# 64-row transposes, strided fills for the gate, zero products and a new instruction order in a block-sparse attention and Fourier-mixing kernel

## The chip, the cores and the metric

The kernel runs on one core of a Trainium2 chip. The metric is the device time of one execution in microseconds. Before the change it is 297.08 us, the median of three runs (296.85 to 297.6).

A core has five engines that work side by side: TensorE (PE in the profile, with its weight loads as a row of its own, PEld), VectorE (DVE), ScalarE (ACT), GpSimd (POOL) and SyncE (SP), which here only issues transfers. Each works off its own queue in order and waits on semaphores for the others. TensorE multiplies into PSUM; the other engines copy from PSUM to SBUF.

## The reference

The program is an attention over selected key blocks, followed by a Fourier-mixing layer with an MLP. Cut to what matters (4 batches, 8 heads, 768 positions, head size 64, model size 512):

```python
# attention, per batch and head; 12 blocks of 64 keys
k_rep = k.reshape(B, H, 12, 64, D).mean(axis=3)
gate = q @ k_rep.T                       # 768 x 12
gate = where(block_of_query >= key_block, gate, -1e9)
selected = top 3 blocks of gate, and the query's own block
scores = 0.125 * q @ k.T, where selected and causal, else -1e9
attn_out = softmax(scores) @ v
# mixing, per batch, on x = heads side by side (768 x 512)
mixed = real(fft over model axis of fft over sequence axis of x)
u = x + mixed
un = (u - mean) / sqrt(var + 1e-6)
out = u + relu(un @ w_ch1) @ w_ch2       # 512 -> 2048 -> 512
```

## The kernel before, in words

Two heads make a pair; there are 16 pairs, four to a batch. Pairs 0 to 6 (P below `NX` = 7) and pairs 7 to 15 take two forms of the same stages, told below.

**Loads and transposes.** `load` brings q and k of a pair in fp32 as six blocks of 128 positions by 128 columns (two heads of 64). `a_tp` (line 286) turns each with a TensorE transpose into a PSUM tile `tp` of 128 by 768: six products of 128 rows per tile (line 292), two tiles per pair. `a_sums` (line 297) sums the keys by block of 64 on VectorE, `a_half` puts the sums into the weights of the gate, `a_k` copies the keys to fp16 on ScalarE (lines 308, 311), `a_q32` copies the queries to fp32 on VectorE (line 316), and `a_q` casts them to fp16 on GpSimd.

**Gate.** `g_mm` multiplies queries with block sums, in four groups of 32 columns of the array. `g_turn` transposes the result on VectorE to the tile `gt`, and bounds the blocks that lie ahead of the query: for pairs 0 to 6 by a minimum with a table `lim` (line 351), for the later pairs by three strided fills. `g_max` finds the eight largest values of each row in nine or ten instructions. `g_less` has two steps: j = 0 writes 1 where a block is below the third largest (`is_lt`), and j = 1 multiplies by a table `oth` or `oth2` that holds -60000 everywhere but at the query's own block. So the mask `lt` is 0 for a block that counts and -60000 for one that does not. `g_back` transposes it back to `mt`.

**Scores.** `s_mm` computes six PSUM tiles of scores per pair, up to two banks each, that hold scores transposed (keys on the partitions). For pairs 0 to 6 each head's product takes 64 rows of the array, the two heads on the two halves (line 409), and the mask is added by more 64-row products with an indicator of blocks, `indz` (line 421). For the later pairs `stage_K` copies the mask beside the queries on GpSimd, and one product of 96 rows does both (line 414). `s_exp` is the exponential on ScalarE (line 431), `s_sel` cuts the causal triangle on GpSimd, `v_mm` multiplies with v and a column of ones in 42 products (line 449), and `v_x` divides, on VectorE, into the tile `x_b` of the batch.

**Mixing.** For each batch `fold_s`, `fold_d` and `fg` fold the sequence and model axes by symmetry on VectorE; `y_mm` and `m_mm` are the two transforms; `m_u` adds x, `m_x` centres and scales it on ScalarE. For batch 0 `t_mm` transposes it on TensorE (24 products, line 585) and `t_copy` copies it to `unT` on VectorE; for the other batches a DMA does this. `w1_mm` then makes 16 tiles `h` of the hidden layer (eight products each, lines 629 and 631), `w1_relu` brings them to SBUF, `w2_mm` multiplies with w_ch2 (lines 648 and 656), `w2_o` adds u on VectorE and `w2_out` stores.

**Order.** All of this is issued in an order that is written out by hand as the string `ORDER`: each word is a step and its arguments (`tk:4` the transposes of pair 4's keys, `s:3,2` its score tile 2, `w:1,5` a tile of W1 in batch 1). `WORK` maps words to functions. Each engine's queue holds its instructions in this order. All PSUM tiles come from one pool of four buffers of two banks each (`pst`), so that a step which takes a new tile waits until the tile four before it is read out.

Of the kernel before, what the change touches and what calls it, by code (L numbers as in the profile page):

```python
# [11 lines left out]
FP = mybir.dt.float32  # L12
F16 = mybir.dt.float16
# [15 lines left out]
def _consts_np():  # L29
# [22 lines left out]
    oth = np.where(np.arange(9)[:, None] + 3 != nn, NEG, 0.0)[None].repeat(128, 0)  # L52

    lim = np.where(nn[None, 4:8] > np.arange(3, 7)[:, None], -3e38, 3e38)
    lim = lim.reshape(1, 16).repeat(128, 0).astype(np.float32)

    indc = np.zeros((4, 32, 2, NB), np.float32)
    for g in range(4):
        for n in range(NB):
            indc[g, n, g % 2, n] = 1.0  # L60

    own = 2 * np.arange(5)[None, :] + 2 + (p // 64)[:, None]
    oth2 = np.zeros((128, 5, 2, 16), np.float32)
# [47 lines left out]

ORDER = """
Lk:1 Lq:1 Lk:2 Lq:2 tk:0 ks:0 tq:0 Lq:3 Lk:3 kh:0 qc:0 iz:1 tk:1 qs:0 kc:0 g:0 ks:1 iz:0 gt:0 tq:1
kc:1 gx:0 Lq:4 Lv:0 Lk:4 Lv:1 kh:1 gl:0,0 tk:2 gl:0,1 gm:0 kc:2 qc:1 s:0,3 s:0,2 ks:2 e:0,3 qs:1
tq:2 Lq:5 Lk:5 s:0,5 qc:2 g:1 e:0,5 e:0,2 kh:2 s:0,4 gt:1 qs:2 s:0,0 e:0,4 gx:1 s:0,1 d:0,2 tq:3
gl:1,0 e:0,0 gl:1,1 tk:3 gm:1 e:0,1 d:0,0 qc:3 g:2 d:0,3 kc:3 d:0,5 s:1,5 gt:2 d:0,4 s:1,0 e:1,5
qs:3 ks:3 s:1,4 e:1,0 tq:4 d:0,1 gx:2 vc:0 e:1,4 s:1,3 qc:4 s:1,1 Lv:2 e:1,3 s:1,2 gl:2,0 kh:3
tk:4 gl:2,1 e:1,2 d:1,3 gm:2 g:3 d:1,4 ks:4 d:1,0 v:0 d:1,5 gt:3 vc:1 kc:4 gx:3 e:1,1 s:2,5 Lv:3
Lq:6 LF:0 Lq:7 Lk:6 Lk:7 LT:0 s:2,3 kh:4 gl:3,0 e:2,5 gl:3,1 s:2,4 e:2,3 d:1,1 x:0 tq:5 qs:4 e:2,4
g:4 d:2,3 gm:3 qc:5 s:2,0 d:2,4 s:2,2 d:1,2 e:2,0 gt:4 d:2,5 tk:5 vc:2 gx:4 e:2,2 s:2,1 ks:5 d:2,0  # L120
Lv:4 Lq:8 Lk:8 s:3,1 e:2,1 v:1 gl:4,0 kh:5 gl:4,1 kc:5 d:2,1 gm:4 d:2,2 s:3,2 x:1 e:3,1 vc:3 g:5
e:3,2 Lv:5 Lc:0 d:3,1 s:3,5 gt:5 s:3,0 fs:0,1 e:3,5 s:3,3 d:3,2 gx:5 e:3,0 s:3,4 fs:1,1 tq:6
gl:5,0 e:3,3 fs:0,0 v:2 gl:5,1 fs:1,0 e:3,4 d:3,3 qc:6 d:3,0 s:4,5 x:2 d:3,4 s:4,4 e:4,5 d:3,5
s:4,0 qs:5 v:3 e:4,0 gm:5 fs:2,0 fs:2,1 e:4,4 s:5,5 x:3 s:4,1 e:5,5 s:5,1 e:4,1 fd:2,0 s:4,2 s:5,0
fs:3,1 e:5,1 fs:3,0 s:5,2 fd:2,1 e:5,0 fd:3,1 s:4,3 fd:3,0 e:5,2 tk:6 f:0,1 f:0,2 e:4,3 Lk:9 Lq:9
tk:7 f:0,3 e:4,2 f:0,0 y:0,1 ks:7 pg:0 W:0 kc:6 y:0,0 tr:0,1 d:4,0 kc:7 d:4,4 d:4,5 ks:6 d:5,5
d:4,1 ty:0,1 tr:0,0 s:5,3 d:5,2 s:5,4 d:4,3 kh:6 W:1 ty:0,0 m:0,2 qs:6 e:5,3 u:0,2 m:0,1 vc:4
e:5,4 m:0,0 u:0,1 xu:0,2 d:5,4 tk:8 d:5,1 d:4,2 u:0,0 xu:0,1 d:5,0 xt:0,2 W:2 g:6 un:0,2 xu:0,0
xt:0,1 gt:6 tq:8 un:0,1 kc:8 xt:0,0 qc:8 tq:7 un:0,0 qs:8 v:4 Lq:10 Lk:10 Lv:6 Lq:11 qc:7 bn:0,3
w:0,4 d:5,3 qs:7 bn:0,1 w:0,5 r:0,4 gx:6 ks:8 w:0,6 r:0,5 gl:6,0 kh:7 gl:6,1 x:4 w:0,7 r:0,6 gm:6  # L130
w:0,3 r:0,7 s:6,5 r:0,3 s:6,1 e:6,5 s:6,3 e:6,1 kh:8 s:6,2 fs:4,0 bn:0,4 w:0,2 e:6,2 d:6,1 X:0
e:6,3 g:7 w:0,0 d:6,5 gt:7 r:0,2 d:6,3 vc:6 gx:7 s:6,4 r:0,0 vc:5 s:6,0 e:6,4 tk:9 Li:0 gl:7,0
Lv:7 tq:9 gl:7,1 e:6,0 gm:7 w:0,11 Lq:12 Lv:8 K:7 qc:9 kc:9 g:8 r:0,11 v:5 gt:8 d:6,0 ks:9 w:0,8
qs:9 gx:8 w:0,10 x:5 r:0,8 d:6,4 d:6,2 gl:8,0 s:7,5 s:7,2 r:0,10 kh:9 fs:4,1 w:0,1 bn:0,5 e:7,5
vc:7 e:7,2 tq:10 gl:8,1 Lv:9 r:0,1 X:1 gm:8 s:7,4 qc:10 w:0,15 d:7,2 e:7,4 K:8 bn:0,0 g:9 r:0,15
s:7,0 w:0,9 gt:9 e:7,0 gx:9 vc:8 tq:11 r:0,9 d:7,0 Lv:10 s:7,1 qc:11 d:7,5 tk:10 d:7,4 e:7,1
gl:9,0 s:7,3 ks:10 v:6 e:7,3 kh:10 gl:9,1 kc:10 gm:9 d:7,3 s:8,4 bn:0,2 d:7,1 w:0,12 vc:9 x:6
e:8,4 K:9 Lv:11 Lk:11 Lq:13 Lq:14 Lk:12 Lk:13 v:7 r:0,12 g:10 x:7 s:8,3 w:0,13 e:8,3 gt:10 nv:0
s:9,4 r:0,13 fs:5,1 s:9,1 fs:7,0 vc:11 w:0,14 e:9,4 fs:6,1 e:9,1 fs:7,1 s:8,1 fs:6,0 fs:5,0
c:0,2,0 r:0,14 fd:7,1 fd:6,1 e:8,1 gx:10 s:9,0 fd:7,0 s:9,2 e:9,0 fd:6,0 s:8,2 gl:10,0 c:0,3,0  # L140
f:1,3 e:9,2 f:1,2 e:8,2 gl:10,1 f:1,0 s:8,0 gm:10 s:9,3 d:8,2 e:8,0 y:1,1 d:8,1 d:9,0 e:9,3 nr:0
c:0,0,0 tr:1,1 ty:1,1 s:9,5 c:0,2,1 e:9,5 d:8,0 d:9,3 tk:11 K:10 s:8,5 c:0,1,0 Lk:14 ks:11 kc:11
c:0,3,1 f:1,1 d:9,5 e:8,5 d:9,1 qs:10 tq:12 o:0,2 y:1,0 od:0,2 kh:11 d:8,4 o:0,3 pg:1 vc:10 qc:12
c:0,1,1 od:0,3 ty:1,0 d:9,4 Lv:12 Lv:13 qs:11 tr:1,0 g:11 c:0,0,1 gt:11 d:8,3 d:8,5 gx:11 qs:12
m:1,0 o:0,0 m:1,1 od:0,0 o:0,1 d:9,2 od:0,1 v:8 u:1,1 m:1,2 u:1,0 xu:1,1 c:0,4,0 gl:11,0 xu:1,0
un:1,1 x:8 s:10,3 gl:11,1 un:1,0 c:0,4,1 u:1,2 e:10,3 d:10,3 fs:8,0 s:10,5 s:10,2 bn:1,3 e:10,5
tk:12 e:10,2 fs:8,1 v:9 gm:11 Lk:15 Lq:15 ks:12 xu:1,2 K:11 bn:1,0 tq:13 kc:12 un:1,2 c:0,5,0
qc:13 vc:13 bn:1,4 s:11,2 d:10,5 x:9 s:11,4 vc:12 e:11,2 c:0,5,1 bn:1,1 Lv:14 Lv:15 e:11,4 s:11,0
o:0,5 s:11,5 w:1,11 e:11,5 od:0,5 o:0,4 e:11,0 kh:12 bn:1,5 od:0,4 s:11,3 w:1,7 e:11,3 r:1,11
s:10,1 d:11,3 r:1,7 d:11,0 s:10,0 e:10,1 d:11,4 g:12 d:10,2 tk:13 d:11,5 e:10,0 gt:12 d:11,2  # L150
s:11,1 ks:13 d:10,1 w:1,0 e:11,1 d:10,0 kh:13 fs:9,0 fs:9,1 s:10,4 r:1,0 d:11,1 gx:12 w:1,14
e:10,4 gl:12,0 gl:12,1 g:13 gm:12 r:1,14 d:10,4 w:1,12 K:12 gt:13 kc:13 gx:13 w:1,6 bn:1,2 r:1,12
tq:14 gl:13,0 r:1,6 qs:13 v:10 qc:14 gl:13,1 s:12,3 gm:13 s:12,5 v:11 x:10 e:12,3 K:13 e:12,5
s:12,0 x:11 w:1,8 e:12,0 fs:10,0 vc:15 s:12,1 r:1,8 s:12,2 fs:10,1 s:13,4 e:12,1 d:12,3 w:1,5
fs:11,1 d:12,5 e:13,4 fs:11,0 d:12,1 fd:10,0 w:1,10 r:1,5 fd:11,0 fd:10,1 s:13,0 fd:11,1 r:1,10
w:1,4 f:2,0 e:13,0 f:2,2 s:13,1 f:2,1 e:12,2 w:1,2 e:13,1 tk:14 r:1,4 w:1,3 ks:14 r:1,2 f:2,3
kc:14 s:12,4 kh:14 r:1,3 pg:2 y:2,0 d:13,4 vc:14 nv:1 e:12,4 qs:14 w:1,9 tr:2,0 w:1,13 ty:2,0
d:12,0 r:1,9 g:14 r:1,13 y:2,1 gt:14 gx:14 s:13,2 w:1,1 e:13,2 gl:14,0 gl:14,1 gm:14 s:13,5 w:1,15
tr:2,1 e:13,5 r:1,1 d:13,5 d:13,0 tk:15 ty:2,1 r:1,15 d:12,4 d:12,2 c:1,0,0 kc:15 nr:1 m:2,0 m:2,1
u:2,0 c:1,1,0 d:13,1 K:14 u:2,1 tq:15 ks:15 xu:2,1 s:13,3 bn:2,3 c:1,0,1 xu:2,0 un:2,1 qc:15  # L160
# [23 lines left out]
def kernel(  # L184
# [603 lines left out]
```

## Time and profile before

| | |
|---|---|
| Median of three runs | 297.08 us (296.85 to 297.6) |
| The profiled execution's own time | 297.41 us |
| Its span, first to last instruction | 295.6 us |
| TensorE busy | 286.5 us (97%), 2633 products |
| VectorE busy | 192.5 us (65%) |
| ScalarE busy | 164.2 us (56%) |
| GpSimd busy | 111.1 us (38%) |
| Granted TensorE clock, mean | 1.00 |
| Moved by DMA | 33.53 MB, 113 GB/s over the span |

A row of a group of instructions reads: line of the program, engine, operation, what is written from what is read, shape, how many; then the busy time and the mean duration of one in ns; then the idle time of that engine just before them, with what ended it. A row of the timeline begins with the start and the length in us, and merges neighbours of one kind (x6 are six instructions). [...] two products of 256 columns are 0.27 us long each and start 0.11 us apart. So TensorE's rate is read from one start to the next.

A row of busy times by stretch has the stretch, its length, the busy time of PE, PEld, DVE, ACT and POOL with the number of instructions, the mean granted TensorE clock, the share of the DMA engines that was in use and the rate in GB/s.

### The profile page before, as it was taken

The page shows a single profiled execution, that of the slowest core. Times are in us where ns is not written, and L with a number is a line of the kernel's source. Part 1 is how long each engine was busy: PE and PEld are TensorE (multiplying, and loading weights), DVE is VectorE, ACT ScalarE, POOL GpSimd, SP SyncE. Part 2 cuts the span into 40 slices and gives each one's busy share as a digit, 9 for nine tenths or more (in the row PEclk, how much of TensorE's full clock was granted, in tenths as well). Part 3 has the DMA queues.
Part 4 walks back from the last instruction along what each step waited for, and adds up shares of the span by engine and source line. Part 5 has one row for each costly group of instructions (what it writes and reads, how often), then busy time and mean ns, then how long its engine had stood idle before and what let it go on. Part 6 is the DMA issues. An engine that isn't in the chain of part 4 may idle for free.

```text
span 295.6 us, 6738 instructions
## 1 busy us (share of the span) xinstructions
PE 286.5 (97%) x2633; PEld 180.2 (61%) x2633; DVE 192.5 (65%) x597; ACT 164.2 (56%) x205; POOL 111.1 (38%) x286
## 2 busy tenths in 40 slices
PE   8899999999999999999999999999999999999995
PEld 4566767765676556656757667446666554555453
DVE  2999999986988638987796577714493282700132
ACT  3698989749578841677788843165524250155000
POOL 2267528528776289064753363220303000110000
PEclk9999999999999999999999999999999999999999
DMA  8999999997999727477000005311000052300023
GB/s 197 268 228 230 262 245 199 195 230 118 226 185 211 168 55 186 118 164 176 3 0 2 0 9 136 38 72 71 2 1 2 32 103 44 142 0 2 0 91 125
DMA packets 93200, 33.53 MB, mean 113 GB/s; under 512 B 85936, under 2 KB 89968, under 8 KB 93168
## 3 DMA queue, kind: packets, MB, share of 16 engines
q1 hardware_dynamic: 87504, 28.47, 40.6%
q0 software_dynamic: 3664, 4.19, 9.1%
q10 hardware_dynamic: 2000, 0.44, 0.7%
q8 instruction: 21, 0.34, 0.5%
q14 instruction: 11, 0.09, 0.1%
HBM read 28.63 MB, written 6.29 MB: 118 GB/s over the span
## 4 chain that ended last, share of the span: by engine, by line
PE 84%; DVE 7%; ACT 6%; DMA 1%; issue 1%; DVEq 0%; ACTq 0%
PE c L656 26%; PE h L629 19%; PE h L631 10%; PE sc L414 7%; PE av L449 6%; ACT pt L431 5%; PE tp L292 5%; PE yp L519 2%; PE mx L552 2%; DVE q L316 2%; PE mx L553 1%; PE warmps L693 1%; DVE u L566 1%; PE g L342 1%; PE c L648 1%; PE sc L409 1%
## 5 line engine op out<-in xcount | busy, mean ns | idle before, releaser
L431 ACT ACTIVATE pt<-sc 128x1024 f16<-128x1024 f32 (+1 forms) x96 | 83.3, 923 | 26.6 <-PE sc L414 19.7
L629 PE MATMUL h<-unT,w 128*128 128x512 f16 x256 | 85.1, 379 | 0.0
L656 PE MATMUL c<-w_sb,hT 128*128 128x512 f16 x368 | 83.8, 379 | 0.0
L631 PE MATMUL h<-unT,w 128*128 128x256 f16 x256 | 69.7, 272 | 0.4 <-DMA unT<-x 0.4
L641 ACT ACTIVATE hT<-h 128x768 f16<-128x768 f32 x48 | 37.8, 813 | 43.7 <-PE h L631 43.7
L656 PEld LDWEIGHTS <-hT 128*128 128x128 f16 x368 | 35.6, 98 | 39.3 <-issue 0.5
L437 POOL TENSOR_SCALAR_AFFINE_SELECT pt<-pt 128x256 f16<-128x256 f16 x96 | 37.5, 414 | 58.5 <-ACT pt L431 57.6
L629 PEld LDWEIGHTS <-w 128*128 128x128 f16 x256 | 25.0, 97 | 29.2 <-issue 1.3
L668 DVE SCALAR_TENSOR_TENSOR u<-c,rs,u 128x512 f32<-128x512 f32 (+1 forms) x25 | 17.5, 725 | 31.2 <-PE c L656 30.4
L639 DVE TENSOR_SCALAR hT<-h 128x768 f16<-128x768 f32 x16 | 15.3, 955 | 29.7 <-PE h L631 29.6
L578 ACT ACTIVATE x<-u,nm 128x512 f16<-128x512 f32 x24 | 15.9, 715 | 22.5 <-DVE nm L572 22.3
L292 PE MATMUL tp<-id,nat 128*128 128x128 f32 x192 | 27.5, 284 | 0.6 <-ACT pt L431 0.3
L631 PEld LDWEIGHTS <-w 128*128 128x128 f16 x256 | 25.0, 98 | 4.3
L225 POOL TENSOR_SCALAR_AFFINE_SELECT qk<-mt 32x160 f16<-32x160 f16 x72 | 23.1, 341 | 10.8 <-DVE mt L386 9.1
L414 PE MATMUL sc<-qk 96*128 96x512 f16 (+3 forms) x144 | 26.8, 305 | 0.0
L225 POOL TENSOR_SCALAR_AFFINE_SELECT qk<-q 64x768 f16<-64x768 f32 (+1 forms) x25 | 20.6, 825 | 14.8 <-DVE q L316 14.1
L292 PEld LDWEIGHTS tp<-id,nat 128*128 128x128 f32 x192 | 22.2, 146 | 5.7 <-issue 1.6
L449 PE MATMUL av<-v,pt 128*128 128x65 f16 x672 | 23.0, 193 | 0.1
L449 PEld LDWEIGHTS <-pt 128*128 128x128 f16 x672 | 22.0, 97 | 1.7 <-POOL pt L437 0.5
L297 DVE TENSOR_REDUCE kr<-tp 128x12 f32<-128x768 f32 x16 | 15.1, 945 | 5.9 <-PE tp L292 5.9
L222 POOL TENSOR_TENSOR t<-vr,rs 128x6 f32<-128x6 f32 x12 | 2.4, 199 | 43.5 <-DVE rs L609 42.9
L414 PEld LDWEIGHTS <-qk 96*128 96x128 f16 x144 | 13.3, 97 | 8.9 <-issue 0.5
(95 smaller groups left out, 351.2 us busy)
## 6 DMA issues: line engine op xcount, KB each, us to landing
nat<-in_v_dram SPq DMA_DIRECT2D x16, 384.0 KB, 4.7
nat<-in_k_dram SPq DMA_DIRECT2D x31, 192.0 KB, 3.5
nat<-in_q_dram SPq DMA_DIRECT2D x31, 192.0 KB, 3.9
out_dram<-u SPq DMA_DIRECT2D x23, 256.0 KB, 2.1
w_sb<-in_moe_w_ch_dram POOLq DMA_DIRECT2D x2, 1024.0 KB, 10.2
w<-in_moe_w_ch_dram POOLq DMA_DIRECT2D x2, 768.0 KB, 8.4
fs_sb<-c_FS SPq DMA_DIRECT2D x1, 582.0 KB, 5.1
w<-in_moe_w_ch_dram POOLq DMA_DIRECT2D x1, 512.0 KB, 7.3
```

Of the source, the lines that this page charges most:

```text
L225: nc.gpsimd.affine_select(out=out, in_=in_, pattern=[[0, i] for i in n], base=0, channel_multiplier=0, compare_op=ALU.is_ge, fill=0.0)
L292: nc.tensor.transpose(ps[:, 128 * st:128 * st + 128], src[:, st, :], id32)
L414: nc.tensor.matmul(ps[:, e, co:co + q1 - q0], qk[0:96, e, 1, 128 * jt:128 * jt + 128], qk[0:96, e, 0, q0:q1], start=True, stop=True)
L431: nc.scalar.activation(out=d["pt"][:, o:o + 2 * n].rearrange("p (e c) -> p e c", e=2), in_=d["sc", i][:, :, 0:n], func=AF.Exp, scale=0.125)
L437: nc.gpsimd.affine_select(out=dg, in_=dg, pattern=[[0, 2], [1, 128]], base=0, channel_multiplier=-1, compare_op=ALU.is_ge, fill=0.0)
L449: nc.tensor.matmul(av[:, e, 66 * st:66 * st + 65], pt[:, co:co + 128], vv[:, e, jt, 0:65], start=(cnt == 0), stop=(cnt == 20))
L578: nc.scalar.activation(out=x_b[:, 2 * kp + k2, :], in_=u_b[:, k2, :], func=AF.Identity, scale=0.0625, bias=nm[:, k2:k2 + 1])
L629: nc.tensor.matmul(hp[:, 0:512], w1s, unT[:, dt, 0:512], start=(dt == 0), stop=(dt == NDT - 1))
L631: nc.tensor.matmul(hp[:, 512:768], w1s, unT[:, dt, 512:768], start=(dt == 0), stop=(dt == NDT - 1))
L641: nc.scalar.activation(out=hT, in_=hp, func=AF.Relu)
L656: nc.tensor.matmul(c_ps[b, g[0]][:, st - g[0], :], h_t[b, it][:, 128 * st:128 * (st + 1)], w2_sb[:, it, :], start=(it == 0), stop=(it == N ...
L668: nc.vector.scalar_tensor_tensor(out=o, in0=ps, scalar=st_t[b][1][:, st:st + 1], in1=o, op0=ALU.mult, op1=ALU.add)
```

## The change

1. `a_tp`: from pair 3 on (`NT` = 3), each block of 128 rows is transposed as two halves of 64 rows, one after the other in the queue, on the two halves of the array. The halves write to different PSUM banks, so the columns of `tp` lie in another order, and `a_sums`, `a_k` and `a_q32` read them through the view `tp_view`. `t_mm` does the same for batch 0, and `t_copy` there becomes two copies per tile.
2. The gate: `g_turn` bounds the coming blocks of pairs 0 to 6 with one strided fill in place of the minimum with `lim`. `g_less` step 0 now fills the own blocks with 3e38 (one strided fill, or two for the later pairs), and step 1 is the `is_lt`. The mask is 0 or 1, and the factor -60000 is in the indicators `indc` and `ind`. The tables `lim`, `oth` and `oth2` and their loads are gone.
3. Zero products: the word `z:n` makes the next PSUM tile begin with n products of a zero tile `zf` of 128 by 128, which the tile's own products overwrite. There are nine such words, 63 products together (12, 15, 4, 6, 5, 4, 4, 8, 5), all ahead of the first tile of W1.
4. `ORDER` is another one throughout.

```diff
-            indc[g, n, g % 2, n] = 1.0
+            indc[g, n, g % 2, n] = NEG
...
-        ind[e, 16 * e:16 * e + NB] = nn[:, None] == (s[None, :] // 64)
+        ind[e, 16 * e:16 * e + NB] = np.where(nn[:, None] == s[None, :] // 64, NEG, 0.0)
...
+    NT = 3
...
     def pst(shape, name, dtype=FP):
-        return psump.tile(shape, dtype, tag="ps", name=name)
+        t = psump.tile(shape, dtype, tag="ps", name=name)
+
+        for _ in range(fill[0]):
+            nc.tensor.matmul(t[:, 0, 0:128] if len(shape) == 3 else t[:, 0:128], zf, zf, start=True,
+                             stop=True, skip_group_check=True)
+        fill[0] = 0
+        return t
...
-        d["tp", who] = ps = pst([128, S], f"tp{who}_{P}")
+        d["tp", who] = ps = pst([128, 2, 512], f"tp{who}_{P}")
         src = nat[P, who].rearrange("p st e d -> p st (e d)")
         for st in range(NST):
-            nc.tensor.transpose(ps[:, 128 * st:128 * st + 128], src[:, st, :], id32)
+            if P < NT:
+                nc.tensor.transpose(ps[:, st // 4, 128 * (st % 4):128 * (st % 4) + 128], src[:, st, :], id32)
+                continue
+            for h in range(2):
+                rows = slice(64 * h, 64 * h + 64)
+                nc.tensor.transpose(ps[:, h, 64 * st:64 * st + 64], src[rows, st, :], id32[rows, rows])
+
+
+    def tp_view(P, who):
+        ps = pairs[P]["tp", who]
+        if P < NT:
+            return ps.rearrange("p h n -> p (h n)")[:, 0:S].rearrange("p (st h c) -> p st h c", h=2, c=64)
+        return ps[:, :, 0:64 * NST].rearrange("p h (st c) -> p st h c", c=64)
...
     def g_turn(P):
         d = pairs[P]
+        d["gt"] = gt = apool.tile([128, 304], FP, tag="gt", name=f"gt_{P}", bufs=1)
         if P < NX:
-            d["gt"] = gt = apool.tile([128, 288], FP, tag="gt", name=f"gt_{P}", bufs=1)
-            nc.vector.transpose(out=gt, in_=d["g"])
-            x = gt.rearrange("p (b n) -> p b n", n=32)[:, 0:4, 4:8]
-            tt(x, x, lim, ALU.min)
+            nc.vector.transpose(out=gt[:, 0:288], in_=d["g"])
+
+            nc.vector.memset(gt[:, 4:136].rearrange("p (b c) -> p b c", c=33)[:, :, 0:4], -3e38)
             return
...
     def g_less(P, j):
...
         if j == 0:
-            tt(l, gt, mx[:, :, 2:3].to_broadcast([128, 9 if P < NX else 10, NB]), ALU.is_lt)
-        else:
-            tt(l, l, o, ALU.mult)
+            if P < NX:
+                nc.vector.memset(gt[:, 3:300].rearrange("p (b c) -> p b c", c=33)[:, :, 0:1], 3e38)
+            else:
+                for h in range(2):
+                    nc.vector.memset(gt[64 * h:64 * h + 64, 2 + h:172 + h]
+                                     .rearrange("p (b c) -> p b c", c=34)[:, :, 0:17:16], 3e38)
+            return
+        nj, w = (9, 32) if P < NX else (10, 16)
+        l = lt if P < NX else ltb.rearrange("p b e n -> p (b e) n")
+        tt(l[:, :, 0:NB], gt[:, 0:nj * w].rearrange("p (j n) -> p j n", n=w)[:, :, 0:NB],
+           mx[:, :, 2:3].to_broadcast([128, nj, NB]), ALU.is_lt)
...
     def t_mm(b, kp):
-        t_ps[b, kp] = ps = pst([128, NDT, 256], f"xt{kp}_{b}", F16)
-        for k2 in range(2):
-            for dt in range(NDT):
-                nc.tensor.transpose(ps[:, dt, 128 * k2:128 * k2 + 128],
-                                    x_t[b][:, 2 * kp + k2, 128 * dt:128 * dt + 128], id16)
+        t_ps[b, kp] = ps = pst([128, 2, 2 * NDT, 128], f"xt{kp}_{b}", F16)
+        for dt in range(NDT):
+            for k2 in range(2):
+                for h in range(2):
+                    rows = slice(64 * h, 64 * h + 64)
+                    nc.tensor.transpose(ps[:, h, dt, 64 * k2:64 * k2 + 64],
+                                        x_t[b][rows, 2 * kp + k2, 128 * dt:128 * dt + 128],
+                                        id16[rows, rows])
```

In the order, the stretch from the last centring of batch 0 to its first W1 tile, before and after (the words of TensorE, VectorE and ScalarE around it; `xu` is the centring, `xt` and `un` the transposes into `unT`, `w` a W1 tile):

```diff
-xu:0,0 xt:0,1 gt:6 tq:8 un:0,1 kc:8 xt:0,0 qc:8 tq:7 un:0,0 qs:8 v:4 ... qc:7 bn:0,3 w:0,4
+xu:0,1 s:6,5 s:6,0 x:5 xt:0,2 e:6,5 e:6,0 z:5 s:6,3 un:0,2 s:6,4 e:6,3 xt:0,1 kh:7 g:7 un:0,1
+e:6,4 d:6,3 s:6,1 gt:7 d:6,5 s:6,2 fs:4,0 e:6,1 d:6,0 w:0,1
```

## The prediction

> **What bounds the kernel now.** I read the stretches of the span first, then the groups of TensorE, the chain of waits and the timeline. The busy times by stretch (PE, PEld, DVE, ACT, POOL in turn) split the run in two at 58.60 us, where the first W1 product of batch 0 starts:
>
> ```profile
> 12.63:55.90 43.27, 40.58 (x635) 29.66 (x632) 41.04 (x137) 40.27 (x51) 24.88 (x50) 1.00 1.06 232
> 58.60:291.90 233.30, 232.92 (x1890) 141.93 (x1886) 141.28 (x428) 117.06 (x146) 82.40 (x217) 1.00 0.37 83
> ```
>
> Ahead of the split VectorE is busy 95% and ScalarE 93%: they set the pace[...]. Behind it TensorE hardly idles, while VectorE and ScalarE have 39% and 50% to spare: TensorE is the bound, so what it saves there comes off the end. The chain of waits agrees: ScalarE and VectorE stand in it up to 56 us, then almost only TensorE.
>
> The timeline of TensorE, behind the split, prices its work:
>
> ```profile
> 79.53 0.27 PE L631 MATMUL h<-unT,w 128*128 128x256 f16 x1
> 79.64 0.82 PE L292 MATMUL tp<-id,nat 128*128 128x128 f32 x6
> 80.30 0.60 PE L414 MATMUL sc<-qk 96*128 96x512 f16 x2
> ...
> 81.93 0.27 PE L631 MATMUL h<-unT,w 128*128 128x256 f16 x1
> 82.13 0.48 PE L342 MATMUL g<-q,krb 128*32 128x160 f32 x8
> 82.54 0.60 PE L414 MATMUL sc<-qk 96*128 96x512 f16 x2
> ```
>
> Start to start, six 128-row fp32 transposes take 0.655 us: 0.109 each, or 0.85 ns a column, and nothing is lost on entering or leaving (the 256-column h product before them gets its usual 0.11). The 32-column gate products do lose on both sides: h to g is 0.20 instead of 0.11, and g to sc 0.41 instead of 0.27 (two passes of 160 columns). In the start times of all such pairs the change of array shape costs 93 to 96 ns each way, to the 64-row shape too; 96 rows count as full.
>
> The 64-row shape is in the timeline at 33 us:
>
> ```profile
> 33.22 0.39 PE L409 MATMUL sc<-qk 64*128 64x512 f16 x2
> 33.45 0.30 PE L421 MATMUL sc<-mt,indz 64*128 64x160 f16 x4
> ```
>
> Two products of 512 columns on the two halves of the array take 0.39 us together; one alone takes 0.38. They overlap.
>
> [...] The trace agrees for fp16 halves (records 4 ns apart) and, by columns, for fp32 (the gate's four, 6 ns apart); 64-row fp32 transposes are in no trace here. [...]
>
> **The change, part by part.**
>
> *Transposes.* 13 pairs, two tiles each, go from 6 blocks to 12 half blocks. A half streams 64 columns, 0.055 us; two halves overlapped, with a little for the weights of 128 columns, 0.058 (estimate). A tile is 6 x 0.058 = 0.35 us instead of 0.655: -0.31. If the halves do not overlap at all, 12 x 0.057 = 0.68: +0.03. I take the first, because fp16 halves overlap so, and fp32 column tiles do. But a 64-row tile in the late stage stands among full-shape products and pays two changes, 0.19, so an isolated one nets only -0.12. Counted in the instruction order of both programs, the shape changes 56 times before (22 behind the first W1 product) and 89 after (43). The batch-0 xt transposes (24 of 0.056 to 24 pairs of 0.03) lie in the early stage and pay for their own changes: nothing.
>
> *Late stage, 233.3 us.* Transposes: 14 tiles x 0.655 = 9.17 become 15 x 0.35 = 5.2: -3.95. Shape changes: 21 more x 0.094 = +1.97. The new order puts pair 6's scores (2.1 us by width), pair 5's 42 av products (1.28) and one gate (0.27) ahead of the first W1 product: -3.6. Sum -5.6: 227.7 us. The waits left in this stage (1.7 us after widths and changes) I keep; the loads and DMA transposes of later batches have more W2 products in front of the next W1 than before.
>
> *Early stage.* By width TensorE has 42.3 us of products and 34 changes (3.2) in the 57.3 us from 1.3 to 58.60, so 11.8 us of waits. After, it has 44.7 us, 3.5 of them the 63 zero products (0.056 each), and 46 changes (4.3): 49.0. That the moved scores and the zeros cost nothing needs the waits: they are there if the stage lasts 60 us or more. So VectorE and ScalarE decide.
>
> VectorE, up to the last copy into unT: off come 7 lim minima (309 to some 65 ns, the mean of the existing strided fills) and 6 own-block products (215 to 65): -2.6. On come the x steps of pairs 4 and 5 (2 x 1.18), pair 8's key sums (0.95), pair 7's halving (0.22), pair 6's gate (max 0.72, fill and compare 0.33, turn back 0.47), and the split unT copies (three of 0.68 to three pairs of 0.4): +5.4. Net +2.8, or 2.6 at the 92% to which the records of back-to-back instructions overlap. ScalarE: pair 8's key copies (2 x 0.8) now precede the last xu, and behind it four exps of pair 6 (0.40 and 3 x 1.04) must free PSUM before scores that stand ahead of W1 in TensorE's queue; then come those scores, 0.6. That is 4.1 us from the last xu to W1 where it was 58.60 - 55.89 = 2.7, while the last xu is itself 2.2 later behind VectorE: +3.6. Between the two: the first W1 product at 61.7, +3.1.
>
> The removed tables (lim, oth, oth2) are small loads that nothing waits for. W1's first chunk is issued some 3 us later on GpSimd's queue, behind selections and q copies, and lands 7.3 us after that, near 56: covered by the later start. The new reading pattern of tp (runs of 64 columns from two banks in turn) I cost at nothing, as the av scaling reads PSUM in runs of 64 too and takes 0.957 us for 768 columns against 0.945 of a plain q copy. The other end are the interleaved reads of yp, tr and ty, at 1.01 on VectorE and 1.04 on ScalarE (a plain key copy is 0.80): 11 early tiles at +0.07 to +0.24 are 0.7 to 2 us more, which I leave to the range. At the head, the 12 zeros ahead of the second q tile and the q copy before the gate turn give back the 0.3 us that the shorter gate saves.
>
> *Sum.* -5.6 + 3.1 = -2.5 us on the profiled span of 295.6. The tail (last W2 half, one addition, the store) keeps its form. The profiled execution took 297.41, the median is 297.08; the difference taken off the median gives 294.6 us.
>
> **Rivals.**
> *The early stage does not stretch.* If VectorE's 2.5 us of idle time and the shorter gate absorb the moved work, W1 starts near 59 and the time is 297.1 - 5.6 + 0.5 = 292. For it: the moved scores are not on W1's data path. Against: the queues above are in order.
> *The early stage eats it all.* If the zeros' 3.5 us are not covered either, W1 starts at 64 to 65 and the time is 296.5 to 298. It decides from +5.6 us, at 64.2. For it: four engines wait on each other there, 8 zero products stand directly before pair 4's av, and each zero group before 64-row scores adds two shape changes.
> *The halves run one after the other.* At 0.114 a pair a late tile costs 0.68 + 0.19: 15 x 0.33 = 5 us more than forecast, 299.6 us, slower than before. Break-even is at 2.5 / (15 x 6) = 0.028 above my 0.058: 0.086 us a pair. For it: only fp16 rows have been seen overlapping, and an fp32 weight load has records of 140 ns against 97. Against: the gate's fp32 tiles start 6 ns apart.
>
> **How the numbers follow.** Forecast 0.50 (293.2 to 296), no stretch 0.20 (291 to 293.2), all eaten 0.20 (296 to 298.8), no overlap 0.10 (298.8 to 301). The range 291.2 to 298.4 leaves out the last case and the edges of two. A difference under 0.3% (0.9 us) can't be told from none. Faster, under 296.2: the first two and a little of the third, 0.71. Same, 296.2 to 298.0: 0.11. Slower: the last case and the end of the third, 0.18.
>
> **What would show it.** Right: six pairs of half transposes in about 0.35 us, with some 0.09 on either side among full-shape products; the strided fills near 65 ns; the first W1 product at 61 to 63 us; from there 227 to 229 us to the last W2 product; clock 1.00 throughout. Wrong: pairs of halves above 0.086; a first W1 product after 64 or before 60; more than 2 us of new waits behind it, say on unT or w; tp copies clearly above 0.95 us.

## The result and the profile after

The changed kernel takes 306.5 us (median of four executions, 304.27 to 307.97) beside 297.34 us for the kernel before on the same chip: a ratio of 1.030, 95% interval 1.023 to 1.037. It is slower by 9 us where the forecast had it faster by 2.5, and above the whole range. The profiled execution took 306.69 us with a span of 305.0 us. Here and below a median is that of all executions of a kernel, and a ratio uses those within 1.5% of its fastest.

The busy times of the changed kernel by stretch (PE, PEld, DVE, ACT, POOL, then the clock, the DMA share and the rate), cut where its own first and last products of the MLP stand:

```profile
12.63:62.90 50.27, 44.07 (x877) 32.57 (x877) 47.12 (x159) 43.93 (x55) 26.94 (x51) 1.00 1.11 214
65.60:300.60 235.00, 230.59 (x1884) 136.51 (x1882) 139.16 (x401) 113.17 (x142) 84.02 (x213) 0.99 0.37 81
```

Both parts of the forecast are off. The first W1 product starts at 65.60 us (58.60 before, 61.7 forecast). From there to the last W2 product it takes 235.0 us (233.3 before, 227.7 forecast), with TensorE busy for 2.3 us less than before, but idle for 4.4 us instead of 0.4, and at a clock of 0.99.

The timeline of TensorE shows a tile of 64-row transposes:

```profile
88.27 0.27 PE L649 MATMUL h<-unT,w 128*128 128x256 f16 x1
88.48 0.59 PE L294 MATMUL tp<-id,nat 64*128 64x64 f32 x12
89.00 0.60 PE L426 MATMUL sc<-qk 96*128 96x512 f16 x2
```

Twelve half transposes take 0.52 us to the next product's start, where six whole ones took 0.655. The halves do overlap, but the product ahead takes 0.21 us instead of 0.11: together 0.73 instead of 0.765.

The waits of TensorE behind the first W1 product (what waited, for what, us in total, times, the longest):

```profile
PE sc L426 <- DVE hT L657: 2.1, 1, 2.1
PE c L674 <- DVE u L686: 1.3, 1, 1.3
PE sc L426 <- DVE kr L306: 0.6, 1, 0.6
PE c L674 <- DVE gt L364: 0.2, 1, 0.2
```

All four wait for VectorE, the engine with 39% to spare. The longest, in TensorE's timeline:

```profile
160.06 0.60 PE L426 MATMUL sc<-qk 96*128 96x512 f16 x2
162.74 0.60 PE L426 MATMUL sc<-qk 96*128 96x384 f16 x4 [2.08 <-DVE hT L657]
163.27 0.86 PE L294 MATMUL tp<-id,nat 64*128 64x64 f32 x12
164.06 0.61 PE L647 MATMUL h<-unT,w 128*128 128x512 f16 x1
164.46 0.42 PE L649 MATMUL h<-unT,w 128*128 128x256 f16 x1
```

and VectorE's at the same time:

```profile
158.10 1.87 DVE L221 TENSOR_TENSOR sd<-x 128x384 f16<-128x384 f16 x2
159.90 0.33 DVE L398 STREAM_TRANSPOSE mt<-ltb 128x160 f16<-128x160 f16 x1
160.16 1.66 DVE L221 TENSOR_TENSOR zw<-sd 128x768 f16<-128x768 f16 x2
161.74 0.94 DVE L657 TENSOR_SCALAR hT<-h 128x768 f16<-128x768 f32 x1
```

The score tile needs the PSUM buffer that the activation hT reads out. That activation stands on VectorE behind four fold instructions (sd, zw). After the wait an h product of 512 columns takes 0.40 us to the next start (164.06 to 164.46) instead of 0.22: the granted clock was halved from 163.4 to 166.8 us. In this trace the stretch of half clock lasts 3.413 us, and those of full clock ahead of it and behind it last 157.01 and 136.53 us, 46.00 and 40.00 times as long; in the trace of the kernel before, the one stretch of full clock lasts 290.13 us, 85.00 times as long. Counted back from the halving in steps of 3.413 us, the step ahead of it (159.95 to 163.36 us) holds the whole wait: TensorE idles in it for 2.08 us, and in every other step between 3 and 299 us for 1.49 us at most. What makes the clock fall, the traces do not show.

The loads changed too. The rates by slice of a fortieth of the span and queue 1 (packets, MB, share of 16 engines' span), of the kernel before:

```profile
GB/s 197 268 228 230 262 245 199 195 230 118 226 185 211 168 55 186 118 164 176 3 0 2 0 9 136 38 72 71 2 1 2 32 103 44 142 0 2 0 91 125
q1 hardware_dynamic: 87504, 28.47, 40.6%
```

and of the changed kernel:

```profile
GB/s 168 218 205 216 192 266 215 193 217 216 198 197 209 136 177 171 122 155 71 0 3 0 2 2 69 69 37 138 4 0 2 51 86 71 104 0 2 0 37 170
q1 hardware_dynamic: 87360, 28.43, 43.3%
```

For about as many packets they take more time. Between 5 and 19 us the mean packet of 256 bytes takes 25.2 ns instead of 18.0 (over the first 30 us 23.0 instead of 18.0; the first packets of all, near 2 us, take 17.8 in both), and the rate of the first two slices falls from 197 and 268 GB/s to 168 and 218. The loads of q and k themselves are the same. But the tiles that they fill moved in SBUF: with the tables gone and the zero tile added, they begin 160 bytes past a multiple of 256 and no longer on one.

### The profile page after: what moved, and what is told of

Its sections match the earlier page's. It is cut to its first block, busy times and chain, and to the rows that moved or that the text cites. A ratio compares the mean times of both kernels' runs of the same rounds, so it can differ in the third digit from the quotient of the medians.

```text
span 305.0 us, 7232 instructions
## 1 busy us (share of the span) xinstructions
PE 287.8 (94%) x2876; PEld 177.3 (58%) x2876; DVE 195.0 (64%) x601; ACT 163.9 (54%) x205; POOL 115.6 (38%) x286
## 4 chain that ended last, share of the span: by engine, by line
PE 69%; DVE 12%; DMA 7%; POOL 5%; ACT 2%; SPq 2%; issue 1%; DVEq 0%; POOLq 0%
PE c L674 22%; PE h L647 17%; PE h L649 8%; PE sc L426 5%; PE av L461 5%; DMA nat<-in_q_dram 3%; PE tp L294 3%; DMA nat<-in_k_dram 3%; POOL qk L224 2%; DVE zw L221 2%; PE yp L531 2%; PE sc L421 1%; DVE fg L221 1%; DVE sd L221 1%; PE c L666 1%
## 5 line engine op out<-in xcount | busy, mean ns | idle before, releaser
L647 PE MATMUL h<-unT,w 128*128 128x512 f16 x256 | 86.5, 384 | 0.0
L659 ACT ACTIVATE hT<-h 128x768 f16<-128x768 f32 x48 | 37.5, 811 | 46.5 <-PE h L649 35.4
L449 POOL TENSOR_SCALAR_AFFINE_SELECT pt<-pt 128x256 f16<-128x256 f16 x96 | 40.9, 446 | 54.5 <-ACT pt L443 53.6
L647 PEld LDWEIGHTS <-w 128*128 128x128 f16 x256 | 25.2, 98 | 29.9 <-issue 2.2
L649 PEld LDWEIGHTS <-w 128*128 128x128 f16 x256 | 25.3, 99 | 4.4
L578 DVE SCALAR_TENSOR_TENSOR u<-mx,x 128x512 f32<-128x512 f32 x24 | 15.6, 686 | 13.6 <-PE mx L565 7.1
L224 POOL TENSOR_SCALAR_AFFINE_SELECT v<-nat 128x768 f16<-128x768 f32 x16 | 14.8, 928 | 9.1 <-DMA nat<-in_v_dram 6.4
L326 DVE COPY q<-tp 128x768 f32<-128x768 f32 x16 | 15.3, 954 | 4.5 <-POOL qk L224 2.0
```

The costliest lines, as they stand in the source:

```text
L224: nc.gpsimd.affine_select(out=out, in_=in_, pattern=[[0, i] for i in n], base=0, channel_multiplier=0, compare_op=ALU.is_ge, fill=0.0)
L449: nc.gpsimd.affine_select(out=dg, in_=dg, pattern=[[0, 2], [1, 128]], base=0, channel_multiplier=-1, compare_op=ALU.is_ge, fill=0.0)
L578: nc.vector.scalar_tensor_tensor(out=u_b[:, k2, :].rearrange("p (m two) -> p two m", two=2), in0=mps[:, k2, :].rearrange("p (two m) -> p t ...
L647: nc.tensor.matmul(hp[:, 0:512], w1s, unT[:, dt, 0:512], start=(dt == 0), stop=(dt == NDT - 1))
L649: nc.tensor.matmul(hp[:, 512:768], w1s, unT[:, dt, 512:768], start=(dt == 0), stop=(dt == NDT - 1))
L659: nc.scalar.activation(out=hT, in_=hp, func=AF.Relu)
```

## The experiments

Three suspects stood out: the new order, the addresses, and the new operations themselves. All times are medians; ratios are to the kernel before on the same chip, with 95% intervals.

### The new operations and the new order, one at a time

The changed kernel without its zero products:

```diff
-z:12 tq:1 ... z:15 tk:2 ... z:5 s:6,3
+tq:1 ... tk:2 ... s:6,3
```

> The changed kernel without its 63 zero products; all else and the order as changed. Theory A (the new order of the work is what costs: q and k arrive late in the early stage, and VectorE and GpSimd fall behind TensorE in the late one): the zeros stand in waits, so 305 to 307 us, as with them. Theory B (the zero products cost: 3.5 us of products and eight changes of array shape): 302 to 303. Theory C (the new forms of the operations cost: half transposes, views, fills): 305 to 307.

Measured: 308.69 us, 1.035 (1.029 to 1.041). This is above all three ranges, and furthest from that of theory B. By the medians the zeros are worth 2.2 us in this order, but the intervals of the two kernels overlap; at any rate they don't cause the loss. In this profile the clock is halved from 59.5 to 62.9 us and the first W1 product comes at 67.10 us.

The new operations in the old order, without zeros:

```diff
-ORDER = """ ... the new one
+ORDER = """ ... the one of the kernel before
```

> The new operations (64-row transposes, strided fills, 0-1 masks) in the order of the kernel before, without zero products. Theory A: by width and shape changes TensorE has 1.8 us less behind the first W1 product, and VectorE some 2.6 us less ahead of it, so 294 to 296 us. Theory C: 302 or more, near the changed kernel. Theory B says nothing against 294 to 296.

Measured: 298.77 us, 1.005 (1.003 to 1.007). The first W1 product stands at 60.10 us, the stage behind it takes 232.1 us, and the packets 25.2 ns (between 5 and 19 us, as in all that follows). The time lies between the ranges of the theories A and C.

The new order with the old operations, without zeros:

> The operations of the kernel before in the new order, without zero products. Theory A: the loss stays or grows, 305 to 310 us. Theory C: 297 to 299. Theory B: 297 to 300.

Measured: 309.06 us, 1.037 (1.034 to 1.041), with the packets at 18.0 ns, the first W1 product at 66.12 us and, behind it, the waits for hT (2.1 us) and u (1.3 us) that the changed kernel has. So the order alone loses as much as the whole change, and the slow packets belong to the new operations, not to the order.

The new operations with the old order up to the first W1 tile and the new one behind:

> The new operations; everything up to the first W1 product in the order of the kernel before, all that is left in the new order, no zero products. Theory A: the first W1 product starts at 57 to 59 us, so the 7 us lost ahead of it come back, and the waits behind it stay: 298 to 301 us. If the waits behind it only follow from the late start, 293 to 296. Theory C: 303 or more.

Measured: 308.7 us, 1.037 (1.034 to 1.039). This cut was a poor one: words of the new order that had not been issued yet, the scores of pair 6 among them, pile up ahead of W1, and its first product comes at 68.34 us instead of the expected 57 to 59. It tells nothing on the late part.

### The addresses

A tile of 96 unused bytes a partition puts the load tiles of the new operations back on a multiple of 256:

```diff
     half = ctile([128, 2, NB], FP, "half")
+    ctile([128, 48], F16, "pad")
```

In the old order:

> The new operations in the old order, without zero products, plus one unused SBUF tile of 96 bytes per partition behind `half`, so that the tiles which q and k are loaded into begin at a multiple of 256 bytes again (as in the kernel before; without it they begin 160 bytes past one, because the tables are gone). Theory D (the lost alignment slows every q and k packet from 17.8 to 25.1 ns, and that eats what the operations save): packets at 17.8 ns again, 294 to 296.5 us. Theory C (the operations themselves save nothing): as without the tile, 298 to 299.5.

Measured: 296.51 us, 0.994 (0.992 to 0.996): 2.3 us less than without the pad, and the packets back at 18.0 ns. In the changed kernel with its zeros and its order:

> The changed kernel with the same 96 bytes. Theory A and D together: the loads are on time again but the order's own cost stays, 302 to 305 us. If the slow loads are the whole loss: 293 to 297. If they play no part: 306 to 307.

Measured: 305.32 us, 1.024 (1.022 to 1.027), packets at 18.0 ns. The 1.2 us are in the expected direction, but the intervals of the two kernels overlap. In the profiled execution the first W1 product comes no earlier, at 65.80 us: a wait of 1.5 us for q near 39 us is gone, but the transform y:0,1 now waits 2.0 us for the gate's `gt:6` where it waited 0.8, and the clock is halved from 46.5 to 49.9 us:

```profile
46.31 1.97 PE L532 MATMUL yp<-fs_sb,fg 128*128 128x193 f16 x12 [2.02 <-DVE gt L361]
```

The counter-proof is the kernel before, with its load tiles moved to where the changed kernel has them, by a tile of 160 bytes in the same place:

> The kernel before, with one unused tile of 160 bytes a partition ahead of the load tiles, so that they begin 160 bytes past a multiple of 256, as in the changed kernel. Nothing else differs. If where the load tiles begin is what made the 256-byte packets of the changed kernel slower (25.1 ns against 17.8 ns), the mean packet reads about 25 ns here too, the first W1 product moves back by 1 to 2 us from 58.60 us, and the time is 298.5 to 300 us. If the slower packets come from anything else in the change (the fills, the new order, the removed tables), they stay at 17.8 ns and the time at 297.3 to 297.7 us.

Measured: 299.61 us, 1.006 (1.004 to 1.008). Its rates and its queue 1:

```profile
GB/s 164 217 205 216 237 243 203 228 164 202 212 201 222 217 49 165 130 164 191 0 3 0 2 0 115 65 72 70 2 1 2 7 118 53 141 0 2 0 90 124
q1 hardware_dynamic: 87504, 28.47, 44.2%
```

The first four slices are those of the changed kernel to within 4 GB/s, its packets take 25.3 ns, and the first W1 product moves from 58.60 to 61.06 us, while the stage behind keeps its 233.1 us. Addresses alone cost 2 us, all of them in the early stage. (The pad moves every tile behind it, those of W1 too; the packets of 256 bytes are what the trace shows of it.) It is the target in SBUF that is off a multiple of 256 bytes here, and the price is 25 ns instead of 18 for packets of 256 bytes.

### Which half of the order

From here on all kernels have aligned load tiles. The old order up to the first W2 product, then the new one, without zeros:

> The new operations, aligned, no zeros: the old order up to the first W2 product of batch 0, what is left in the new order. Theory A, late part (GpSimd and VectorE fall behind in batches 1 and 2): 2 to 5 us above the aligned operations in the old order, 297 to 300. If the late waits only follow from the early delay: no more than 1 us above.

Measured: 305.37 us, 1.022 (1.016 to 1.027). The first W1 product stands at 57.22 us, but TensorE waits again for hT (2.1 us) and u (1.3 us), and for 2.1 us more for kr close behind the seam, where the two orders don't meet well. With these the time is above the expected 297 to 300 us. The new order up to the first W2 product, zeros included, then the old one:

> The new operations and the zeros, aligned: the new order up to the first W2 product of batch 0, what is left in the old order. Theory A, early part: first W1 product at 64 to 66 us and 4 to 6 us above the aligned operations in the old order, 299 to 302. If the early delay comes from the slow loads alone: 294 to 297.

Measured: 300.03 us, 1.009 (1.006 to 1.011). Its stretch from the first W1 to the last W2 product:

```profile
63.87:293.32 229.45, 228.39 (x1883) 135.54 (x1882) 137.34 (x401) 113.17 (x142) 82.30 (x213) 1.00 0.34 80
```

The stage takes 229.45 us at full clock, where the new order takes 233.8. By the medians the new order loses 5.3 us (305.32 to 300.03) behind the first W2 product. In the profiles 4.4 us are in this stage; the first W1 product is earlier too (63.87 instead of 65.80 us), though the order ahead of it is the same. TensorE waits 2.0 us for `gt:6` in both, but here the clock stays full:

```profile
46.11 1.18 PE L531 MATMUL yp<-fs_sb,fg 128*128 128x193 f16 x12 [2.02 <-DVE gt L360]
```

This kernel's remaining 3.5 us over the old order throughout (296.51) come from the part ahead of the first W2 product.

### The late waits

One word moved, `r:1,3`, the activation that reads out tile 3 of the hidden layer of batch 1, so that this activation of the long wait stands ahead of the folds:

```diff
-s:13,0 ... (folds, a layer norm, a compare) ... r:1,3
+s:13,0 r:1,3 ... (folds, a layer norm, a compare)
```

> The changed kernel with its load tiles aligned (305.3 us), with one item of the order moved: the third-expert hidden activation r:1,3 on VectorE stands right behind s:13,0 instead of behind the fold, layer-norm and rank work queued ahead of it. If the 2.26 us wait of TensorE near 161 us, and the half clock of 3.4 us that follows it, come from that queue, both go and the time is 301 to 303.5 us. If the wait only moves to the next place (the score tile waits for another release), the time stays at 304.5 to 305.5 us.

Measured: 303.6 us, 1.019 (1.016 to 1.023). The wait at 161 us is gone, and a wait of 0.8 us of a gate product for its weights `krb`, up to 166.3 us, takes a part of its place. The half clock behind the wait, which I had named, is not in the profile of the aligned kernel: there the wait, 2.1 us long too, lies across two of the steps of 3.413 us, counted from that kernel's own halving at 46.5 us, with about 1.3 us in the first. Its half clock stands at 46.5 us, and that of this kernel at 48.3. The second wait, for u near 130 us, hangs on the stores of batch 0: VectorE may not write a new u before the old one is stored (in the changed kernel it waits 4.2 us for that), and SyncE's queue has the store behind a value load and transposing transfers.

```diff
-c:0,1,1 Lk:15 ... c:0,2,0 o:0,0 K:11 xu:1,1 Lv:14 od:0,0 o:0,1 m:1,2 ks:12 un:1,1 od:0,1
+c:0,1,1 o:0,0 od:0,0 o:0,1 od:0,1 Lk:15 ... c:0,2,0 K:11 xu:1,1 m:1,2 ks:12 un:1,1 Lv:14
```

> The changed kernel with its load tiles aligned (305.3 us), with the two output stores of batch 0 that the new order put later (o:0,0 od:0,0 o:0,1 od:0,1) moved ahead to right behind c:0,1,1, and the value load Lv:14 to behind un:1,1. If the 1.37 us wait near 130 us comes from SyncE's queue (the value load, then the store, then the transposing transfer that writes u's buffer free), it goes, and the time is 302.5 to 304.5 us. If it is hidden by or moves to the wait near 161 us, the time stays within 0.5 us of 305.3 us.

Measured: 303.89 us, 1.021 (1.017 to 1.024). The waits at 127 and 130 us are gone; the one for hT is still there.

The other waits have the same form: gt and kr, short readings of a PSUM buffer, stand behind fold sums. All of them together:

```diff
-f:0,1 y:0,1 d:4,1 d:5,0 gt:6
+gt:6 f:0,1 y:0,1 d:4,1 d:5,0
-f:1,2 r:0,9 g:10 vc:9 w:0,14 kc:11 gt:10
+r:0,9 g:10 vc:9 w:0,14 kc:11 gt:10 f:1,2
-f:1,3 c:0,0,0 r:0,14 gl:10,0 ks:11
+ks:11 f:1,3 c:0,0,0 r:0,14 gl:10,0
(and the moves of the two runs before)
```

> The changed kernel with aligned load tiles (305.3 us) and five places of the new order changed, no operation added or removed: gt:6 ahead of f:0,1, f:1,2 behind gt:10, ks:11 ahead of f:1,3, r:1,3 right behind s:13,0, and the stores o:0,0 od:0,0 o:0,1 od:0,1 right behind c:0,1,1 with Lv:14 behind un:1,1. If the new order loses its time in short VectorE operations that free a PSUM bank and stand behind the folds (and in the one store chain), the waits near 46, 100, 130 and 161 us go or shrink to under 0.5 us each, the late stage falls from 233.8 us to 229 to 230.5 us, and the time is 299.5 to 301.5 us. If those waits only move to the next release, the time stays at 302 to 304 us, no better than one of the moves alone (303.6 and 303.9 us).

Measured: 300.03 us, 1.008 (1.006 to 1.009). Its waits of TensorE behind the first W1 product:

```profile
PE g L353 <- DVE krb L220: 0.6, 1, 0.6
PE c L674 <- DVE gt L364: 0.5, 1, 0.5
```

The stage takes 229.93 us instead of 233.82, both at full clock. The first W1 product comes at 64.46 us instead of 65.80: of the 2.0 us for `gt:6`, 1.3 remain, more than the 0.5 expected, but the half clock behind them is gone. Five changed places in an order of over a thousand words, with not one operation added or removed, give back 5.3 us.

### The early stage

In that kernel the first W1 product is still 2.8 us behind the forecast. Its timeline of VectorE during the folds of batch 0:

```profile
43.38 0.70 DVE L220 TENSOR_TENSOR fg<-zw 128x762 f16<-128x762 f16 x1
44.00 0.38 DVE L513 COPY fg<-zw 128x6 f16<-128x6 f16 x1
...
45.56 0.67 DVE L220 TENSOR_TENSOR fg<-zw 128x762 f16<-128x762 f16 x1
...
46.15 0.88 DVE L510 COPY mid<-zw 128x6 f16<-128x6 f16 x1
```

and of GpSimd:

```profile
43.26 2.56 POOL L449 TENSOR_SCALAR_AFFINE_SELECT pt<-pt 128x256 f16<-128x256 f16 x5 [5.73 <-ACT pt L443]
45.77 1.22 POOL L223 TENSOR_SCALAR_AFFINE_SELECT v<-nat 128x768 f16<-128x768 f32 x1
```

A copy of six elements takes 0.38 and 0.88 us here, and 0.17 in the kernel before. There GpSimd stood still during the folds: the word `pg:0`, a copy that waits for the folded tile, stood ahead of the cuts in its queue. In the new order `pg:0` stands 26 words behind the last fold `f:0,0` instead of 3, and the cuts stand ahead of it. The kernel before has a case of the same kind, the `lim` minimum of 16 elements (shortest, median and longest in ns, then the first and the last start):

```profile
L222 DVE TENSOR_TENSOR gt<-gt,lim x7: 174/270/662, 10.2 to 55.5; 128x16 f32<-128x16 f32 x7
```

At 10.2, 33.6 and 55.5 us, with no GpSimd instruction beside it, it takes 174 to 175 ns; the other four times one runs beside it, and it takes 270 to 662 ns. GpSimd held still again, with `W:0`, the first transfer of W1, moved along:

```diff
-d:5,5 f:0,3 d:4,2 e:5,3 gt:6 f:0,1 y:0,1 d:4,1 d:5,0 e:4,4 d:5,3 f:0,0 s:5,2 ... pg:0 W:0
+f:0,3 e:5,3 gt:6 f:0,1 y:0,1 e:4,4 f:0,0 pg:0 W:0 d:5,5 d:4,2 d:4,1 d:5,0 d:5,3 s:5,2 ...
```

> The changed kernel with aligned load tiles and the five moves (300.0 us), and GpSimd held still during the folds of batch 0: pg:0 and W:0 right behind f:0,0, the cuts d:5,5 d:4,2 d:4,1 d:5,0 d:5,3 behind them. If the two-input sums on VectorE are lengthened by GpSimd's cuts beside them, fg falls back to 390 to 420 ns a piece and the copies to 0.17 us, the first W1 product moves from 64.5 us to 62.5 to 63.3 us, and the time is 298.3 to 299.3 us. If they are long for another reason, fg stays above 500 ns and the time at 299.7 to 300.5 us; if fg falls but the first W1 product doesn't move, VectorE is not what paces this stage.

Measured: 303.7 us, 1.021 (1.019 to 1.024): neither of the outcomes that I had written. The sums fg are at 0.54 to 0.56 us. That is what they took in the kernel before (0.55 to 0.56), so the 390 to 420 ns that I had written were wrong. The copies are back at 0.17 us, and the stretch from the first fg to the last copy takes 2.8 us instead of 4.4, so the cuts did lengthen it. Two rows of the sums, of the kernel before and of this one:

```profile
43.17 0.56 DVE L222 TENSOR_TENSOR fg<-zw 128x762 f16<-128x762 f16 x1
43.37 0.56 DVE L220 TENSOR_TENSOR fg<-zw 128x762 f16<-128x762 f16 x1
```

But 3.7 us are lost. VectorE behind the folds:

```profile
47.27 1.02 DVE L550 CAST tr<-yp 128x768 f16<-128x768 f32 x1 [0.35 <-ACT ty L544]
48.19 4.50 DVE L220 TENSOR_TENSOR lt<-gt,mx 128x108 f16<-128x108 f32 x1
52.62 0.94 DVE L306 TENSOR_REDUCE kr<-tp 128x12 f32<-128x768 f32 x1
```

and GpSimd:

```profile
47.25 1.83 POOL L449 TENSOR_SCALAR_AFFINE_SELECT pt<-pt 128x256 f16<-128x256 f16 x5
49.05 0.89 POOL L223 TENSOR_SCALAR_AFFINE_SELECT v<-nat 128x768 f16<-128x768 f32 x1
49.90 1.48 POOL L449 TENSOR_SCALAR_AFFINE_SELECT pt<-pt 128x256 f16<-128x256 f16 x4
51.34 0.82 POOL L223 TENSOR_SCALAR_AFFINE_SELECT qk<-q 128x768 f16<-128x768 f32 x1
52.12 0.77 POOL L739 DMA_DIRECT2D w<-in_moe_w_ch_dram  x1
```

One compare, which takes 0.27 us in the next kernel, lasts 4.50 us. It ends about half a microsecond after GpSimd turns from its back-to-back cuts and copies to issuing a transfer (52.69 and 52.12 us), while one instruction after another had passed before it. That this series held it is a reading of the times; the trace doesn't show what holds an instruction. TensorE then waits 3.8 us for the second `tr` (a copy of the first transform's result, which stands behind the compare), and the clock is halved from 53.6 to 60.4 us. The same compare, its word moved seven places ahead, to where GpSimd issues W1's first transfer:

```diff
-gl:6,0 d:5,1 e:5,2 tr:0,1 d:4,4 tk:7 ty:0,0 d:5,2 gl:6,1
+gl:6,0 gl:6,1 d:5,1 e:5,2 tr:0,1 d:4,4 tk:7 ty:0,0 d:5,2
```

> The kernel with GpSimd held during the folds (303.7 us) and one word moved: gl:6,1, the compare of pair 6, right behind gl:6,0, so that it runs near 47 us while GpSimd issues W1's transfer instead of beside the block of cuts. If GpSimd's cuts are what held the compare for 4.50 us, it takes 0.25 to 0.45 us here, the 3.8 us wait for tr and the half clock at 53.6 us go, the first W1 product stands at 62 to 63.5 us, and the time is 298 to 299.3 us. If another operation is locked out in its place, the first W1 product stays above 64 us and the time at 300 us or more.

Measured: 299.05 us, 1.005 (1.003 to 1.007). VectorE:

```profile
46.42 0.27 DVE L220 TENSOR_TENSOR lt<-gt,mx 128x108 f16<-128x108 f32 x1
```

GpSimd:

```profile
45.73 0.95 POOL L739 DMA_DIRECT2D w<-in_moe_w_ch_dram  x1
46.71 1.83 POOL L449 TENSOR_SCALAR_AFFINE_SELECT pt<-pt 128x256 f16<-128x256 f16 x5
```

and the stretches of this kernel:

```profile
12.63:59.26 46.63, 42.66 (x862) 31.73 (x864) 44.73 (x157) 42.83 (x54) 25.76 (x51) 1.00 1.02 222
61.96:291.91 229.95, 228.76 (x1883) 135.77 (x1882) 139.91 (x401) 112.95 (x142) 84.54 (x213) 1.00 0.35 83
```

The compare is at 0.27 us and the first W1 product at 61.96 us, within 0.3 us of the forecast; the profiled execution is the fastest of eight (297.92 to 299.68). The move of this one word is worth 4.7 us.

### What the operations themselves are worth

The kernel before with the 64-row transposes and the copies that read them, nothing else:

```diff
+            for h in range(2):
+                rows = slice(64 * h, 64 * h + 64)
+                nc.tensor.transpose(ps[:, h, 64 * st:64 * st + 64], src[rows, st, :], id32[rows, rows])
```

> The kernel before with the 64-row transposes of pairs 3 to 15 and of the layer-norm output, and the copies that read them; masks, tables, order and addresses of the load tiles as before. By the forecast's terms the late stage loses 3.95 us of transposes and gains 1.97 us of shape changes, less in the old order, where the transposes stand in other places: 1 to 2 us off 297.6 us, so 295.6 to 296.6 us. If the halves bring nothing beside their shape changes, or TensorE waits for VectorE where they were, 297.3 to 298 us; then the 1 us gain of the old order with all new operations comes from the fills.

Measured: 296.55 us, 0.997 (0.996 to 0.998). That is all that the new operations in the old order reach together (296.51): the fills and masks add nothing that these runs resolve, though VectorE has 1.5 us less to do up to the first W1 product (49.3 instead of 50.8). A gain of the fills may hide behind the clock: in the profiled execution of the old order with all new operations it is halved twice ahead of W1 (43.7 and 57.4 us), and the fastest executions of that kernel take 295.46 us, those of the transposes alone 296.43. So the next kernel tries to keep the clock up: the old order with all new operations and 45 zero products at TensorE's waits between 40 and 58 us:

```diff
+z:5 tk:6  +z:5 tk:7  +z:8 y:0,1  +z:4 m:0,2  +z:8 g:6  +z:6 tq:8  +z:4 v:4  +z:5 tq:7
```

> The old order with the new operations and aligned load tiles (296.5 us), with 45 zero products put at TensorE's waits between 40 and 58 us. If those waits are what halved the clock at 43.7 and 57.4 us in the profile of that kernel, both drops go, the first W1 product comes at 57.5 to 58.5 us, and the time is 294.5 to 296 us in every run. If the zero products only push TensorE's own work back, the time is 296.5 to 298 us.

Measured: 297.36 us, 0.999 (0.998 to 1.000): the time of the second outcome with the signs of the first. In the profile the clock stays full and the first W1 product comes at 57.74 us, as expected, but what is gained there is lost again behind it, with a wait of 1.8 us for unT up to 132.7 us (0.9 us without the zeros). Four of 22 executions took 301.25 to 304.46 us, for which I have no cause. Of all these kernels two are faster than the kernel before by more than the measurement leaves open, both in the old order: the transposes alone (0.3%), and the new operations with the pad (0.6%).

## Why the prediction was wrong

*Transposes.* Right in kind: the halves overlap, and pairs start 62 ns apart (0.058 forecast). The size was off in one term. The first pair of a tile takes 112 ns to the next start and not 58; the trace has the second pair's weight loads begin 57 ns behind the first products. (It is the entry into the shape that costs: a tile directly behind another one starts with a pair of 62 ns.) From the start of the product ahead to the start of the one behind, a tile among full-shape products takes 0.73 us instead of 0.765: a gain of 0.04 us where the forecast had 0.12. Over the 13 such tiles behind the first W1 product this is 1 us of the expected 5.6. The copies that read the tiles kept their times (keys 0.79 us, queries 0.95), and the fills took 66 to 72 ns (65 forecast). The rival "The halves run one after the other" is out.

*Late stage.* The forecast was 227.7 us, and the stage took 235.0. The five moves take off 3.9 us (233.82 to 229.93, both at full clock), and the half clock, which this profile has and that of the aligned kernel has not, stands for about the 1.2 us between 235.0 and 233.82. Without both the new order takes 229.9 (two runs); the 1 us above explains a part of the 2.2 left, and the idle time that remains, 1.2 us instead of 0.4, most of the rest. The step that failed is "The waits left in this stage (1.7 us after widths and changes) I keep". It was a claim on the order, and I had looked at the new order only for what it moves past the first W1 product. Behind it, it also puts the PSUM readings gt, kr and hT behind fold instructions on VectorE, and the stores behind other transfers on SyncE. Those waits and the half clock behind one of them cost about 5 us (3.9 and 1.2) in a stage in which VectorE is busy for 59% of the time. That VectorE and ScalarE have 39% and 50% to spare was read as if they could not hold TensorE up. That does not follow: with four PSUM buffers, one late reading is enough.

*Early stage.* The forecast for the first W1 product, 61.7 us by the balance of VectorE and ScalarE, is what the last kernel gives (61.96) once nothing collides, and its terms hold one by one: the last xu ends 2.1 us later than before (2.2 forecast), and from there to W1 it takes 4.0 us (4.1 forecast). The changed kernel takes the same 4.0 us, so its delay lies wholly ahead of the last xu, which ends at 61.6 us and not at 58.1. None of the rivals names its causes. The durations of fg, mid and lt were taken from the rows of before, where GpSimd stands still beside them. The rows of before also have the lim minimum, at 174 to 175 ns alone and 270 to 662 ns beside GpSimd, and I did not ask which other VectorE instructions the new order would put beside GpSimd's cuts. Of that: 2.5 us on the first W1 product between the kernel with five moves and the last one. Next, the transform y:0,1 waited for gt:6, again a PSUM reading behind folds: 0.8 us in the changed kernel, 2.0 us in the one with aligned tiles, whose first W1 product came 1.3 us earlier once this and the other four places were mended. Last, "The removed tables are small loads that nothing waits for" is true of the loads, but the tables also took space, and without them the targets of the 256-byte packets begin at other addresses. That costs 2 us in the kernel before. What it costs in the changed kernel's early stage is not shown: the profile with aligned tiles has its first W1 product no earlier (65.80 us), with a longer wait for gt:6 and a half clock in place of the wait for q.

*Zeros.* That they cost nothing could not be resolved in the new order; in the old order they did not pay either.

*Rivals and range.* "The early stage eats it all" named the right place, a first W1 product after 64.2, but blamed the zeros, and it still trusted the late stage for −5.6 us. No case held a new wait behind W1, though the section on what would make the prediction wrong names "more than 2 us of new waits". A range to 298.4 us had no room for the 5 us that followed.

*The sum, as the runs show it.* 306.5 us, less about 1.2 (0 to 2.3) for the addresses gives 305.3; less 5.3 for five queue places gives 300.0; less 1.0 for GpSimd beside VectorE (2.5 in the profiled executions, of which the last kernel's is its fastest) gives 299.05. That is still 1.6 us over the kernel before, though in the profiled execution of this last kernel the last W2 product starts at 291.91 us, where it started at 291.86. What else its other executions lose was not tried.

## What to carry to other kernels

A new instruction order is a change of its own, and must be costed queue by queue: for each PSUM buffer, ask which instruction reads it out last, and what stands ahead of that instruction on its engine. Idle share says nothing on that. Before trusting a duration of a VectorE operation from the old profile, look at what GpSimd does beside it then, and what it will do afterwards: here copies of 0.17 us took up to 0.88 us beside its cuts, and a compare of 0.27 us took 4.50. And when a change adds or removes SBUF tiles, compare where the tiles behind them begin.

## What the runs showed of the hardware that I had not expected

- An unused tile of 160 bytes a partition made the kernel 2 us slower, by moving the targets of 256-byte packets off a multiple of 256 bytes: 25 ns a packet instead of 18 between 5 and 19 us.
- A VectorE compare of 0.27 us lasted 4.50 us beside back-to-back GpSimd instructions: cuts, a cast and more cuts passed before it ended.
- Behind a wait of TensorE of 2.1 us the clock was halved for 3.4 us; in the profile of the same kernel with aligned tiles a wait as long, near 161 us, had no half clock behind it. In the first it fell wholly into one step of 3.413 us ahead of the halving, in the second about 1.3 us of it did, in steps counted from that profile's own halving.
- Overlapped 64-row fp32 transposes on the two halves of the array start 62 ns apart a pair, where a whole 128-row block takes 109 ns, but the first pair behind a change of shape gains nothing (112 ns).
